# Gate and value products as seven products of sums, in an mLSTM cell with a SwiGLU block

## The chip, the cores and the metric

The kernel runs on one core of one Trainium2 chip. The metric is device time in microseconds of one launch, as the median of several runs. The engines are TensorE (PE: matrix products into PSUM, with its weight loads shown as PEld), VectorE (DVE), ScalarE (ACT), GpSimd (POOL) and SyncE (SP), which here only issues DMAs.

## The reference

An mLSTM cell over 4 batches x 8 heads x 768 steps of 40 features gives y; its rows are laid out as x with 3072 tokens of 320 features. Then a SwiGLU block follows, in float32 throughout:

```python
g = x @ w_gate                            # 320 x 1536
silu = g * (1.0 / (1.0 + np.exp(-g)))
val = x @ w_val                           # 320 x 1536
return (silu * val) @ w_out               # 1536 x 320
```

The weights arrive in 64 bits and are rounded to float32 in the kernel. q, k, v and the gates arrive as float32.

## The kernel before

The 768 steps are cut into six groups of 128 (g = 0 to 5, called groups one to six in the text). A group has 4 batches x 128 steps = 512 tokens. While the SwiGLU block of group g runs on TensorE, the cell of group g+1 is computed in between and the inputs of group g+2 are loaded. Every engine works through its instructions in the order in which the program names them; there is no planner. Lists of closures (`slots`, by chunk, and `before`, by step of the output product) put the cell's parts between the products.

**Gate and value products** (`hidden`, L646). The 1536 hidden features are 12 chunks m of 128. The 320 input features are five pieces of 64 rows. For each piece a gate product runs in rows 0 to 63 of the array and a value product in rows 64 to 127, side by side, each 512 columns wide (L651). The transposed input `xT` therefore holds every piece in both halves. After ten products ScalarE takes the Silu of the gate (L656) and VectorE multiplies it by the value (L657) into `h_sb`.

**Output product** (`project_seven`, L698, from group two on). h and w_out are halved in hidden features, tokens and outputs, and seven half-size products of sums replace eight (L717). The sums of h come from GpSimd (`out_sums`, L688) and VectorE (`out_fourth`, L693); `out_weights` makes those of the weights once, on GpSimd at the start of group two. The first group uses the plain product `project_all` (L664, L668).

**The cell of the next group**: scores (L331) weighed by VectorE (L338); `add` (L353) and `next_state` (L369), with GpSimd's `decayed` (L362); `attend` (L377, L382), then `gather` on VectorE (L391 to L398), GpSimd's `gate` (L403) and `divide` (L409), which writes x. In the slots these come after chunks 3, 4, 5, 7, 8, 9 and 10.

**Turning x.** From group three on, x is sent as 32x32 squares by 16 DMAs per half (`send_squares`, L418) into `x_sq`, and VectorE transposes the squares (`turn_inputs`, L425, L426) into `xT` during the output product, at steps 4 and 5. For groups one and two TensorE transposes x (`first_seam` L558, `seam` L431).

**SP's queue** issues nearly all DMAs, in program order: q and k as squares after chunk 2 (L315), k after 5 (L117), v and the decay weights (`weights_load`, L444) after 9, the o gate after 10, the squares of x after 8 and 10, and the outputs (L709) in the output product. Weights (`piece_load`, L140) come in ten pieces at the start; of the gate and value pieces, gate rows go to partitions 0 to 63 and value rows to 64 to 127, the values by ScalarE's queue for the first five. They are rounded on ScalarE (L190, L192), VectorE (L199, L200) and GpSimd (L207).

PSUM has eight banks, four under the tag "cell" and four under "gen". `hidden` and the output product use "gen", the cell uses "cell".

Of the kernel before, what the change touches and what calls it, by code (L numbers as in the profile page):

```python
# [18 lines left out]
L = 128  # L19
# [5 lines left out]
def kernel(  # L25
# [35 lines left out]
    PAIRS = [(c, c + 1) for c in range(0, NKC - 1, 2)] + [(NKC - 1, 0)] + [(c, c + 1) for c in range(1, NKC - 1, 2)]  # L61
    assert NG * L == S and NFC == 12 and NFC * 128 == DF and TW == 512 and D <= DP and NKC * HP == DM
# [13 lines left out]
    def bank(name, tag="cell"):  # L76
        return psum.tile([128, 512], F32, name=name, tag=tag)
# [16 lines left out]
    vw_sb = const.tile([128, BH, D1], F32)  # L94
# [3 lines left out]
    xT_sb = const.tile([128, NKC, TW], F32, name="xT")  # L98
# [41 lines left out]
    def piece_load(p, home=None):  # L140
        kind, m, n = PIECES[p]
        if kind == "gv":
            a, d = NKC, n * 128
            src = [(slice(i * HP, (i + 1) * HP), w[:, m * 128:(m + n) * 128].rearrange("(c p) f -> p c f", p=HP))
                   for i, w in enumerate((moe_w_gate, moe_w_val))]
            queues = (nc.sync, nc.scalar if p < 5 else nc.sync)
        else:
            a, d = n, DM
            src = [(slice(0, 128), moe_w_out[m * 128:(m + n) * 128].rearrange("(a p) d -> p a d", p=128))]
            queues = (nc.sync,)  # L150
        if src[0][1].dtype == F32:
            for r, w in src:
                if kind == "o":
                    nc.sync.dma_start(out=wo_sb[r, m:m + n, :], in_=w)
                else:
                    for x in range(n):
                        nc.sync.dma_start(out=wgv_sb[r, m + x], in_=w[:, :, ts(x, 128)])
            return
# [5 lines left out]
        for (r, w), queue in zip(src, queues):  # L164
            queue.dma_start(out=raw[r].rearrange("p (a d) -> p a d", a=a), in_=w.bitcast(U32))
# [239 lines left out]
    def divide(n, P, den):  # L405
        for b in range(2):
            u, r = 2 * P + b, slice(b * H, (b + 1) * H)
            x = x_sb[:, u, 0:DM] if n == 1 else x_all[:, u * DM:(u + 1) * DM]
            nc.vector.tensor_tensor(x.rearrange("p (h d) -> p h d", d=D), o_sb[:, u * H:(u + 1) * H],  # L409
                                    den[:, r].to_broadcast([128, H, D]), op=ALU.mult)  # L410
        if n == 1:
            nc.gpsimd.tensor_copy(x_sb[:, 2 * P:2 * P + 2, DM:], x_sb[:, 2 * P:2 * P + 2, 0:HP])

    x_all = x_sb.rearrange("p u d -> p (u d)")[:, 0:B * DM]

    def send_squares(P):  # L418
        for t in range(L // SQ):
            src = x_all[t * SQ:(t + 1) * SQ, 2 * P * DM:(2 * P + 2) * DM].rearrange("p (w e) -> p w e", e=2 * SQ)  # L420
            for r in range(128 // SQ):
                nc.sync.dma_start(out=x_sq[r * SQ:(r + 1) * SQ, 2 * P * NKC:(2 * P + 2) * NKC, t, :],
                                  in_=src[:, :, (r % 2) * SQ:(r % 2 + 1) * SQ])

    def turn_inputs(n, u):  # L425
        nc.vector.transpose(out=xT(n)[:, :, ts(u, L)], in_=x_sq[:, u * NKC:(u + 1) * NKC].rearrange("p w t d -> p w (t d)"))  # L426
# [4 lines left out]
    def seam(n, P, engs):  # L431
        engs = list(engs)
        dst = xT(n).rearrange("p c (u i s) -> p c u i s", u=B, i=2)
        for cs in (range(0, 4), range(4, NKC)):
            tp = [bank("tp_x")[:, 0:len(cs) * L].rearrange("p (c u s) -> p c u s", u=2, s=SUB) for _ in range(2)]
            for c in cs:
                for b in range(2):
                    for i in range(2):
                        nc.tensor.transpose(tp[i][:, c - cs[0], b, :],  # L439
                                            x_sb[half(i), 2 * P + b, ds(PAIRS[c][0] * HP, 2 * HP)], ident[half(i), half(i)])  # L440
            for i in range(2):
                copy(engs.pop(0), dst[:, cs[0]:cs[-1] + 1, 2 * P:2 * P + 2, i, :], tp[i])
# [98 lines left out]
    def first_gate(P):  # L541
# [3 lines left out]
        nc.gpsimd.tensor_copy(x_sb[:, 2 * P:2 * P + 2, DM:], x_sb[:, 2 * P:2 * P + 2, 0:HP])  # L545
# [12 lines left out]
    def first_seam(P, engs):  # L558
        for c, eng in zip(range(0, NKC, 2), engs):
            cs = range(c, min(c + 2, NKC))  # L560
            tp = bank("tp_x")[:, 0:len(cs) * 2 * L].rearrange("p (c u s) -> p c u s", u=2, s=L)
            for w in cs:
                for b in range(2):
                    nc.tensor.transpose(tp[:, w - c, b, :], x_sb[:, 2 * P + b, ds(PAIRS[w][0] * HP, 2 * HP)], ident)
# [36 lines left out]
    first_seam(0, (A, A, V))  # L601
# [5 lines left out]
    first_seam(1, (A, A, V))  # L607
# [38 lines left out]
    def hidden(g, m, first=()):  # L646
        ps = [bank("gv_ps", "gen") for _ in range(2)]
        x = xT(g)
        for kc in range(NKC):
            for i in range(2):  # L650
                nc.tensor.matmul(ps[i], lhsT=wgv_sb[half(i), m, PAIRS[kc][i] if g < 2 else kc, :], rhs=x[half(i), kc, :],  # L651
                                 start=(kc == 0), stop=(kc == NKC - 1))
# [35 lines left out]
    def out_sums(k, eng):  # L688
        eng.tensor_tensor(S1[:, k], h_sb[:, k, second_half], h_sb[:, KH + k, second_half], op=ALU.add)  # L689
        eng.tensor_tensor(h_sb[:, k, second_half], h_sb[:, k, first_half], h_sb[:, k, second_half], op=ALU.subtract)  # L690
        eng.tensor_tensor(S2[:, k], S1[:, k], h_sb[:, k, first_half], op=ALU.subtract)  # L691

    def out_fourth(eng):  # L693
        for k in range(0, KH, 2):
            a12 = h_sb[:, KH + k:KH + k + 2, first_half]
            eng.tensor_tensor(a12, a12, S2[:, k:k + 2], op=ALU.subtract)

    def project_seven(g, before):  # L698
# [5 lines left out]
        node = {x: bank("o_ps", "gen")[:, 0:DM].rearrange("p (u d) -> p u d", d=NW) for x in "eacdb"}  # L704
# [21 lines left out]
        product("e", a12, lambda k: wo_sb[:, KH + k, n1], True, True)  # L726
        step(1)
        product("a", a11, lambda k: wo_sb[:, k, n1], True, True)
        nc.scalar.copy(u2, node["a"])  # L729
        z = fresh()  # L730
        nc.vector.tensor_tensor(z, u2, node["e"], op=ALU.add)  # L731
        send(z, 0, n1)
        out_fourth(nc.vector)
        step(2)
        product("c", a21, lambda k: wo_sb[:, k, n2], True, False)
        nc.scalar.copy(v, node["c"])
# [4 lines left out]
        product("b", lambda k: S2[:, k], lambda k: wT[:, 1, k], True, True)  # L741
# [86 lines left out]
    def early_squares(part):  # L828
# [12 lines left out]
        4: [run(convert, 16), run(seam, 1, 0, (A, V, A, V))],  # L841
        5: [run(seam, 1, 1, (A, V, A, V)), run(convert, 17), run(weights_sub, 2, 0), run(weights_mask, 0)],
# [9 lines left out]
    k_sq = late.tile([128, PP, L // SQ, SQ], F32, name="k_sq")  # L852
    nc.gpsimd.memset(k_sq, 0.0)
    x_sq = late.tile([128, B * NKC, L // SQ, SQ], F32, name="x_sq")
    wT = late.tile([128, 3, KH, NW], F32, name="wT")
    S1 = late.tile([128, KH, TH], F32, name="S1")
    S2 = late.tile([128, KH, TH], F32, name="S2")
    out_weights(nc.gpsimd)

    for g in range(1, NG):  # L860
        n, f = g + 1, g + 2
        slots = {m: [] for m in range(NFC)}
        if n < NG:
            if n > 2:
                slots[0] = [run(turn_squares, q_sq, qT)]
                slots[1] = [run(turn_squares, k_sq, kT)]
            slots[3] = [run(do_scores), run(do_weigh, 0)]
            slots[4] = [run(do_weigh, 1)]
            slots[4].append(run(do_decayed, 2 * n))
            slots[5] = [run(do_add, n), run(do_state, 2 * n)]  # L870
            slots[7] = [run(do_attend, n, 0), run(do_gather, n, 0)]
            slots[8] = [run(do_divide, n, 0), run(send_squares, 0)]
            slots[9] = [run(do_attend, n, 1), run(do_gather, n, 1)]
            slots[10] = [run(do_divide, n, 1), run(send_squares, 1)]
        if f < NG:
            slots[2] += [run(load_squares, q_sq, q, f), run(load_squares, k_sq, k, f)]
            slots[5].append(run(load_all, k_sb, k, f))
# [47 lines left out]
```

## Time and profile before

| | |
|---|---|
| median of 3 runs | 537.5 us (537.4 to 537.51) |
| the profiled execution | 538.14 us |
| its span, first to last instruction | 536.3 us |
| granted TensorE clock | 1.000 |
| busy: PE, PEld | 529.8 us (99%), 338.8 us (63%) |
| busy: DVE, ACT, POOL | 261.0, 132.1, 182.4 us |
| L651, gate and value products | 1440 instructions, 317.2 us |
| L717, output products | 840 instructions |

The span is the time between the first and the last instruction in one profiled execution; the execution lasts a little longer, and the median of runs lies 0.64 us below that one execution. A float32 product is two instructions on TensorE, so the 720 products of L651 are 1440. Matmul durations overlap: a line's busy time counts a stretch once, its mean duration is that of one instruction alone.

### The profile page before, as it was taken

The numbers are of one execution on the slowest core, as the hardware profiler recorded it, in microseconds if no ns is written. First come the engines' busy times: TensorE is split into PE (matmuls) and PEld (weight loads), VectorE is DVE, ScalarE is ACT, GpSimd is POOL, SyncE is SP. The second block draws the span as 40 slices with busy tenths as digits, with TensorE's granted clock in tenths as the row PEclk, the third lists the DMA queues.
The fourth block names the chain that finished last, engine by engine and source line by source line (L and its number), as shares of the span: only waits on it lengthen the run. The fifth ranks groups of instructions, "written<-read, shape, count | busy, mean of one in ns | idle before, by whom it ended". The sixth has DMA issues, their size and how long they took to land.

```text
span 536.3 us, 12510 instructions
## 1 busy us (share of the span) xinstructions
PE 529.8 (99%) x5349; PEld 338.8 (63%) x5349; DVE 261.0 (49%) x437; ACT 132.1 (25%) x193; POOL 182.4 (34%) x194
## 2 busy tenths in 40 slices
PE   8999999999999999999999999999999999999997
PEld 4964545766745697555598455589455579544496
DVE  5769686982255542545633436635435734111121
ACT  3367555444110114101013210104201010011110
POOL 1303346579216534014627004437003530003410
PEclk9999999999999999999999999999999999999999
DMA  9999997898640496471296353296000131000001
GB/s 125 175 275 197 183 286 144 155 122 125 74 55 1 73 137 116 50 88 17 46 149 131 45 58 51 38 150 113 26 2 2 26 60 41 24 1 0 2 12 38
DMA packets 226879, 45.76 MB, mean 85 GB/s; under 512 B 214824, under 2 KB 221992, under 8 KB 226824
## 3 DMA queue, kind: packets, MB, share of 16 engines
q1 hardware_dynamic: 224916, 42.11, 48.9%
q10 hardware_dynamic: 1908, 2.85, 2.0%
q8 instruction: 42, 0.69, 0.6%
q14 instruction: 13, 0.11, 0.1%
HBM read 35.68 MB, written 4.01 MB: 74 GB/s over the span
## 4 chain that ended last, share of the span: by engine, by line
PE 91%; DMA 4%; SPq 3%; DVE 1%; POOL 0%; issue 0%; DVEq 0%; POOLq 0%
PE gv_ps L651 56%; PE o_ps L717 21%; PE o_ps L668 5%; SPq L117 3%; DMA wo_sb<-in_moe_w_gate_dram 2%; PE inter L377 2%; PE sp L331 2%; PE intra L382 2%; DMA raw<-in_moe_w_gate_dram 2%; PE add L353 2%; PE tp_kq L296 0%; POOL wgv_sb L207 0%; DVE M_sb L281 0%; PE tp_x L439 0%; DVE wgv_sb L200 0%
## 5 line engine op out<-in xcount | busy, mean ns | idle before, releaser
L651 PE MATMUL gv_ps<-xT,wgv_sb 64*128 64x512 f32 x1440 | 317.2, 593 | 0.9 <-DVE wgv_sb L207 0.8
L651 PEld LDWEIGHTS gv_ps<-xT,wgv_sb 64*128 64x128 f32 x1440 | 142.3, 187 | 155.2 <-issue 148.9
L657 DVE TENSOR_TENSOR h_sb<-sg,gv_ps 128x512 f32<-128x512 f32 x72 | 49.4, 686 | 177.3 <-ACT sg L656 177.3
L656 ACT ACTIVATE sg<-gv_ps 128x512 f32<-128x512 f32 x72 | 43.0, 597 | 264.8 <-PE gv_ps L651 264.6
L717 PEld LDWEIGHTS o_ps<-wo_sb,h_sb 128*128 128x128 f32 x480 | 65.6, 190 | 3.8 <-issue 3.8
L717 PE MATMUL o_ps<-wo_sb,h_sb 128*128 128x160 f32 x480 | 67.4, 300 | 0.0
L689 POOL TENSOR_TENSOR S<-h_sb 128x256 f32<-128x256 f32 x30 | 23.2, 773 | 100.9 <-DVE h_sb L657 100.9
L362 POOL TENSOR_TENSOR C<-C,dec 128x328 f32<-128x328 f32 x20 | 14.5, 736 | 114.6 <-DVE C L369 114.6
L456 POOL TENSOR_SCALAR_AFFINE_SELECT w_sb<-w_sb 64x1024 f32<-64x1024 f32 x20 | 28.4, 1421 | 37.1 <-DVE w_sb L451 36.1
L717 PE MATMUL o_ps<-wT,S 128*128 128x160 f32 x240 | 33.4, 299 | 0.0
L717 PEld LDWEIGHTS o_ps<-wT,S 128*128 128x128 f32 x240 | 32.9, 190 | 0.0
L668 PE MATMUL o_ps<-wo_sb,h_sb 128*128 128x320 f32 x96 | 26.9, 437 | 0.0
L690 POOL TENSOR_TENSOR h_sb<-h_sb 128x256 f32<-128x256 f32 x30 | 22.8, 760 | 2.4
L668 PEld LDWEIGHTS o_ps<-wo_sb,h_sb 128*128 128x128 f32 x96 | 17.9, 190 | 7.2
L691 POOL TENSOR_TENSOR S<-S,h_sb 128x256 f32<-128x256 f32 x30 | 21.7, 724 | 0.0
L394 DVE TENSOR_TENSOR y_sb<-y_sb,intra 64x328 f32<-64x328 f32 x40 | 19.7, 492 | 0.7
L369 DVE TENSOR_TENSOR C<-C,add 40x328 f32<-40x328 f32 (+1 forms) x36 | 17.7, 493 | 1.2 <-POOL C L362 0.6
L207 POOL TENSOR_TENSOR wgv_sb<-wgv_sb,low 128x640 int32<-128x640 int32 x6 | 9.3, 1544 | 24.6 <-DVE wgv_sb L200 24.6
L717 PE MATMUL o_ps<-wT,h_sb 128*128 128x160 f32 x120 | 17.1, 299 | 0.0
L731 DVE TENSOR_TENSOR z_sb<-sg,o_ps 128x320 f32<-128x320 f32 x5 | 2.4, 487 | 29.3 <-ACT sg L729 23.5
L426 DVE STREAM_TRANSPOSE xT<-x_sq 128x640 f32<-128x640 f32 x16 | 12.5, 822 | 8.5 <-DMA x_sq<-x_sb 8.5
L717 PEld LDWEIGHTS o_ps<-wT,h_sb 128*128 128x128 f32 x120 | 16.6, 190 | 0.0
(152 smaller groups left out, 471.8 us busy)
## 6 DMA issues: line engine op xcount, KB each, us to landing
w_sb<-M_dram SPq DMA_DIRECT2D x10, 512.0 KB, 11.3
x_sq<-x_sb SPq DMA_DIRECT2D x128, 40.0 KB, 2.0
k_sb<-in_k_dram SPq DMA_DIRECT2D x12, 320.0 KB, 6.0
v_sb<-in_v_dram SPq DMA_DIRECT2D x12, 320.0 KB, 5.8
o_sb<-in_o_gate_dram SPq DMA_DIRECT2D x12, 320.0 KB, 5.5
raw<-in_moe_w_out_dram SPq DMA_DIRECT2D x3, 1280.0 KB, 7.4
q_sb<-in_q_dram SPq DMA_DIRECT2D x32, 64.0 KB, 2.3
out_dram<-z_sb SPq DMA_DIRECT2D x20, 80.0 KB, 2.5
```

Source lines behind the costliest of these rows:

```text
L117: nc.sync.dma_start(out=dst[:, heads(P), 0:D], in_=tokens(a, c, P))
L369: nc.vector.tensor_tensor(c, c, ps[r], op=ALU.add)
L394: nc.vector.tensor_tensor(t, t, intra[i][half(c)], op=ALU.add)
L456: nc.gpsimd.affine_select(w, w, compare_op=ALU.is_ge, fill=NEG, base=0, pattern=[[0, UH], [1, SUB]], channel_multiplier=-1)
L651: nc.tensor.matmul(ps[i], lhsT=wgv_sb[half(i), m, PAIRS[kc][i] if g < 2 else kc, :], rhs=x[half(i), kc, :], start=(kc == 0), stop=(kc == N ...
L656: nc.scalar.activation(sg, ps[0], AF.Silu)
L657: nc.vector.tensor_tensor(hid(g, m), sg, ps[1], op=ALU.mult)
L668: nc.tensor.matmul(ps[u], lhsT=hid(g, m)[:, ts(u, L)], rhs=wo_sb[:, m, :], start=(m == 0), stop=(m == NFC - 1))
L689: eng.tensor_tensor(S1[:, k], h_sb[:, k, second_half], h_sb[:, KH + k, second_half], op=ALU.add)
L690: eng.tensor_tensor(h_sb[:, k, second_half], h_sb[:, k, first_half], h_sb[:, k, second_half], op=ALU.subtract)
L691: eng.tensor_tensor(S2[:, k], S1[:, k], h_sb[:, k, first_half], op=ALU.subtract)
L717: nc.tensor.matmul(node[x][:, i], lhsT=lhs(k)[:, ts(i, L)], rhs=rhs(k), start=start and k == 0 and i == 0, stop=stop and k == KH - 1, skip ...
```

## The change

1. `hidden` (groups one and two) takes 256 features as full-height products of 128 rows, and the remaining 64 as a pair of 64-row products, gate in the upper half of the array and value in the lower. Even chunks end with the pair, odd chunks begin with it. x's last 64 features stand in both halves of `xT`'s third block; the other features are stored once, so `xT` has 3 blocks for 5, the seams transpose 3 for 5, and each square DMA carries 6 for 10 pieces. The weights of a piece come in four DMAs for two.
2. In groups three to six `unit` does chunks k and k+6 together. The 256 features, gate/value and the 512 tokens are halved, and seven 128-row products of 256 columns per chunk replace eight; the 64-row rest is done plainly in 64-row pairs, four products per chunk. ScalarE copies the first node, VectorE adds five times from PSUM and multiplies twice, ScalarE takes two Silus of 512 columns (as before).
3. The weight sums are made once, by GpSimd during group two, after each chunk; two DMAs swap the halves of the 64-row weights. The input sums are five VectorE operations per group, after the turns.
4. The output product has four nodes for five; the sum S2 is formed in place by VectorE (`out_second`).
5. Units and cell steps take the two PSUM tags in turn.
6. Moved: the turns of q and k from chunks 0 and 1 of the next group to step 1 of the output product, and with them k's load; k's squares after chunk 6 for 2; v's load from after chunk 9 to after the second half of x's squares; all four turns of x at step 4.

The diff, cut to its core:

```diff
+        src = [(slice(0, 128), slice(2 * i, 2 * i + 2), w[0:256, cols].rearrange("(c p) f -> p c f", p=128), queue)
+               for i, (w, queue) in enumerate(((moe_w_gate, nc.sync), (moe_w_val, second)))]
+        src += [(half(i), slice(4, 5), w[256:DM, cols].rearrange("(c p) f -> p c f", p=HP), nc.sync)
+                for i, w in enumerate((moe_w_gate, moe_w_val))]
...
     def hidden(g, m, first=()):
...
-        for kc in range(NKC):
-            for i in range(2):
-                nc.tensor.matmul(ps[i], lhsT=wgv_sb[half(i), m, PAIRS[kc][i] if g < 2 else kc, :], rhs=x[half(i), kc, :],
-                                 start=(kc == 0), stop=(kc == NKC - 1))
+        for part in ((0, 1) if m % 2 == 0 else (1, 0)):
+            opens, closes = part == m % 2, part != m % 2
+            for c in range(2) if part == 0 else (2,):
+                for i in range(2):
+                    w, r = (wgv_sb[:, m, 2 * i + c], x[:, c]) if part == 0 else (wgv_sb[half(i), m, 4], x[half(i), 2])
+                    nc.tensor.matmul(ps[i], lhsT=w, rhs=r, start=opens and c != 1, stop=closes and c != 0)
...
+    def out_second(eng):
+        for k in range(0, KH, 2):
+            a11 = h_sb[:, k:k + 2, first_half]
+            eng.tensor_tensor(a11, S1[:, k:k + 2], a11, op=ALU.subtract)
...
+    def weight_sums(ms, eng):
+        w, t = wgv_sb[:, ms], wS[:, ms]
+        eng.tensor_tensor(t[:, :, 0], w[:, :, 2], w[:, :, 3], op=ALU.add)
+        eng.tensor_tensor(t[:, :, 1], t[:, :, 0], w[:, :, 0], op=ALU.subtract)
+        eng.tensor_tensor(t[:, :, 2], w[:, :, 1], t[:, :, 1], op=ALU.subtract)
...
+    def input_sums(eng):
+        x1, x2 = (lambda c: xT_sb[:, c, first_half]), (lambda c: xT_sb[:, c, second_half])
+        eng.tensor_tensor(xT_sb[half(1), 2, second_half], xT_sb[half(1), 2, second_half], xT_sb[half(1), 2, first_half],
+                          op=ALU.subtract)
+        eng.tensor_tensor(xS[:, 0], x2(0), x1(0), op=ALU.subtract)
+        eng.tensor_tensor(xS[:, 1], x2(1), xS[:, 0], op=ALU.subtract)
+        eng.tensor_tensor(x2(0), x2(1), x2(0), op=ALU.subtract)
+        eng.tensor_tensor(xS[:, 2], x1(1), xS[:, 1], op=ALU.subtract)
+
+    def unit(k, tag):
+        ms = (k, KH + k)
+        A4 = [bank("gv_ps", tag).rearrange("p (j t) -> p j t", j=2) for _ in range(4)]
+        na, nb, nd, ne = A4
...
+        rest = xT_sb[:, 2]
+        for two in (((na, 0, wgv_sb[:, :, 4], rest[:, first_half]), (nb, 1, wR, rest[:, second_half])),
+                    ((nd, 0, wR, rest[:, second_half]), (ne, 1, wgv_sb[:, :, 4], rest[:, second_half]))):
+            for j, m in enumerate(ms):
+                for node, i, w, x in two:
+                    nc.tensor.matmul(node[:, j], lhsT=w[half(i), m], rhs=x[half(i)], start=j == 0, stop=False,
+                                     skip_group_check=True)
+
+        def product(node, w, x, stop):
+            for j, m in enumerate(ms):
+                nc.tensor.matmul(node[:, j], lhsT=w(m), rhs=x, start=False, stop=stop, skip_group_check=True)
...
+        product(na, lambda m: wgv_sb[:, m, 0], x1(0), False)
+        nc.scalar.copy(sa, na)
+        product(nb, lambda m: wS[:, m, 1], xS[:, 1], True)
+        nc.vector.tensor_tensor(sa, sa, nb, op=ALU.add)
+        product(nd, lambda m: wgv_sb[:, m, 2], x2(0), False)
+        nc.vector.tensor_tensor(h2, sa, nd, op=ALU.add)
+        product(ne, lambda m: wS[:, m, 0], xS[:, 0], False)
+        nc.vector.tensor_tensor(h2, h2, ne, op=ALU.add)
+        product(na, lambda m: wgv_sb[:, m, 1], x1(1), True)
+        nc.scalar.activation(sg, na, AF.Silu)
+        product(nd, lambda m: wgv_sb[:, m, 3], xS[:, 2], True)
+        nc.vector.tensor_tensor(h1, sa, nd, op=ALU.add)
+        nc.vector.tensor_tensor(h1, sg, h1, op=ALU.mult)
+        product(ne, lambda m: wS[:, m, 2], x2(1), True)
+        nc.vector.tensor_tensor(sa, sa, ne, op=ALU.add)
+        nc.scalar.activation(sa, sa, AF.Silu)
+        nc.vector.tensor_tensor(h2, sa, h2, op=ALU.mult)
+        out_sums(k, nc.gpsimd)
...
     for g in range(1, NG):
...
-            slots[2] += [run(load_squares, q_sq, q, f), run(load_squares, k_sq, k, f)]
-            slots[5].append(run(load_all, k_sb, k, f))
-            slots[9] += [run(load_all, v_sb, v, f), run(weights_load, f)]
-            slots[10].append(run(load_all, o_sb, o_gate, f))
-        for m in range(NFC):
-            hidden(g, m)
-            if m >= KH:
-                out_sums(m - KH, nc.gpsimd)
-            for s in slots[m]:
-                s()
+            slots[2] += [run(load_squares, q_sq, q, f)]
+            slots[6] += [run(load_squares, k_sq, k, f)]
+            slots[9] += [run(weights_load, f)]
+            slots[10] += [run(load_all, v_sb, v, f), run(load_all, o_sb, o_gate, f)]
+        if g == 1:
+            for m in range(NFC):
+                hidden(g, m)
...
+                weight_sums(slice(m, m + 1), nc.gpsimd)
+                weight_difference(slice(m, m + 1), nc.gpsimd)
+            weight_rest(nc.gpsimd)
+        else:
+            for j in range(KH):
+                unit(j, side())
+                for s in slots[2 * j] + slots[2 * j + 1]:
+                    s()
...
-            before[4] += [run(turn_inputs, n, 0), run(turn_inputs, n, 1)]
-            before[5] += [run(turn_inputs, n, 2), run(turn_inputs, n, 3)]
+            before[4] += [run(turn_inputs, n, u) for u in range(B)] + [run(input_sums, nc.vector)]
+            before[1] += [run(turn_squares, q_sq, qT), run(turn_squares, k_sq, kT), run(load_all, k_sb, k, f)]
```

## The prediction

> **What bounds it now.** I read, in this order, the busy table, the chain that ended last, then the timelines of VectorE and of SP's queue over the third group (208.3 to 291.5 us), because the change hands work to exactly those two.
>
> ```profile
> PE 529.8 (99%) x5349; PEld 338.8 (63%) x5349; DVE 261.0 (49%) x437; ACT 132.1 (25%) x193; POOL 182.4 (34%) x194
> PE 91%; DMA 4%; SPq 3%; DVE 1%; POOL 0%; issue 0%; DVEq 0%; POOLq 0%
> ```
>
> TensorE is busy throughout, and beyond the first 46 us the chain stays on it. So each PE microsecond removed counts, until another queue makes PE wait. The chain in order of time (start, length, engine, tile, line, instructions) gives PE's rates:
>
> ```profile
> 99.32 8.81 PE o_ps L668 x32
> 108.13 0.77 PE tp_x L439 x20
> 108.90 2.35 PE o_ps L668 x8
> ...
> 374.74 17.37 PE gv_ps L651 x80
> 392.11 2.02 PE sp L331 x128
> 394.13 8.78 PE gv_ps L651 x40
> ...
> 434.82 23.02 PE o_ps L717 x168
> 457.84 51.70 PE gv_ps L651 x240
> ```
>
> A float32 matmul is two instructions. Take a chunk m of L651 (20 instructions, ten pairs of 64-row halves) as a, a start as t: 240 take 12a+t = 51.70, 80 take 4a+t = 17.37; so a = 4.291 us and **t = 0.205 us**. L668 says the same: 32c+t = 8.81, 8c+t = 2.35, c = 0.2692, t = 0.197. Each such start is a change of how the array is cut (64 rows to 128, or 64x64 to 64x128). For L717, (23.02-0.2)/168 = 0.1358. Hence 135.8 ns at 160 columns, 269.2 at 320 and 429.1 per 64-row pair at 512: a column over 1.2 GHz, plus 2.5 ns. At 256 columns I use **215.8 ns**.
>
> **PE, part by part.** A unit replaces two chunks (8.58 us). It has 16 rest instructions in 8 pairs, 8 x 0.2158 = 1.73, and 7 products of 4, 28 x 0.2158 = 6.04: 7.77 us. It saves 0.81; 24 units (groups three to six) save 19.5 us.
>
> Against that stand the new changes of cut, 0.2 each. Each unit changes once inside (rest to products): 6 per group. The first two units stand side by side, one more; before each cell step a change was there already; the project step now follows 128-row work, one less. That is +1.2 us in groups three to five. Group six has no cell steps: 6+5-1 = 10, +2.0. Together 5.6: **PE net -13.9 us**.
>
> In groups one and two the products stay whole, now 128-row plus a 64-row pair (8 x 0.4292 + 2 x 0.4292 = a again), with a change inside each chunk: 12 x 0.2. Group two saves those at its two ends, less the small rest: +1.8. In group one PE waits for weights up to the fourth chunk (45.9 us), which hides those; eight chunks and the key/query turns remain: +1.9. The seam into group two turns 24 instead of 40 blocks (two 0.77 rows to 0.46): -0.6. The new loading of the weights (four DMAs per piece for two) I take as 0, bounded by +-1.5: the third chunk's weights arrive at 38.1 us and PE waits 0.56 for them; the bytes are the same, but eight outstanding DMAs hold half as many pieces.
>
> A rule of the Trainium skill speaks against the whole plan: "TensorE: Matmul & The Clock Gate", Part 3, The mechanism, says that a weight load overlaps running matmuls only where their row groups differ. By that, 28 loads of 0.19 us would stand bare in each unit, 128 us in all. L717's row contradicts it: 480 full-height loads of 190 ns each, one matmul every 137 ns; the measurement decides.
>
> **VectorE inside a unit.** Rows: 128x512 with a PSUM operand 0.686 (L657; next independent start after 0.61), ScalarE 0.60 (L656). With PE starting at 0, rest and two changes end at 2.13, then 0.863 per product: na 2.99, nb 3.86, nd 4.72, ne 5.58, na 6.45, nd 7.31, ne 8.17. VectorE: first add 3.9-4.6, second 4.75-5.4, third 5.6-6.3; then add, product, add, ScalarE's Silu, product: 7.35 to 10.7. It falls 2.5 us behind PE's end, but its next first add is due at 8.17+3.9 = 12.07. So **units in a row don't stall** (group six). PE needs the second add by 6.45, which is the tight place. Around it stand the cell's steps:
>
> ```profile
> 237.85 4.09 DVE L369 TENSOR_TENSOR C<-C,add 40x328 f32<-40x328 f32 x8
> ...
> 248.20 0.90 DVE L391 TENSOR_TENSOR y_sb<-inter,e_T 128x328 f32<-128x328 f32 x2
> 249.01 2.06 DVE L394 TENSOR_TENSOR y_sb<-y_sb,intra 64x328 f32<-64x328 f32 x4
> 251.11 0.19 DVE L396 SCALAR_TENSOR_TENSOR den<-y_sb 128x16 f32<-128x16 f32 x1
> 251.33 1.34 DVE L397 TENSOR_SCALAR den<-den 128x16 f32<-128x16 f32 x1
> 252.71 0.25 DVE L398 RECIPROCAL den<-den 128x16 f32<-128x16 f32 x1
> ...
> 254.71 1.42 DVE L409 TENSOR_TENSOR x_sb<-o_sb,den 128x320 f32<-128x320 f32 x2
> ```
>
> All of these now queue behind a unit's last product and ahead of the next unit's first add. From group start (PE at 0): third unit ends 26.5, VectorE 29.1; state 4.1 plus GpSimd's decays behind its two sums ends at 33.5; the fourth unit's first add was due at 32.0, its PE stalls 0.4. Fourth unit ends 36.7, gather (0.9+2.06+1.85 from 39.2) 43.8 against 42.5: stall 0.2. Fifth unit ends 47.0, its VectorE 49.5; divide to 50.9, second gather to 55.6 against 52.9: stall 1.6. Sum 2.2 per group, three groups: **+6.5 us** (1 to 4 each). Units end at 58.8, the project step (22.8) at 81.6.
>
> **The seam: SP's queue.** The same queue carries the inputs' squares, the next group's loads and the outputs.
>
> ```profile
> 256.15 11.85 SPq L422 DMA_DIRECT2D x_sq<-x_sb  x16
> 268.11 2.22 SPq L117 DMA_DIRECT2D v_sb<-in_v_dram  x2
> 270.42 3.78 SPq L447 DMA_DIRECT2D w_sb<-M_dram  x2
> 274.30 13.09 SPq L422 DMA_DIRECT2D x_sq<-x_sb  x16
> 287.48 1.67 SPq L117 DMA_DIRECT2D o_sb<-in_o_gate_dram  x2
> 289.25 2.05 SPq L709 DMA_DIRECT2D out_dram<-z_sb  x2
> 291.39 0.85 SPq L709 DMA_DIRECT2D out_dram<-sg  x2
> ```
>
> Before, the last squares are issued at 287.4, VectorE turns them by 290.8 and PE starts the next group at 291.48: 0.7 us to spare. SP had no gap from 256.2 on, so SP, not PE, nearly sets this seam already.
>
> After: the first divide comes after the fifth unit, so squares start at 51.6 (50.9, then GpSimd's copy). 16 issues 11.9 -> 63.5. Then the weights' two loads and 16 issues: 16.9 as above with v's two loads queued ahead of them; these are moved behind, so 13.4 (2.2 for two loads on an empty queue, as v's row, and 16 x 0.657+0.7). End T = 76.9. Landing 1.9 (median 2.0), two turns 1.0, first of the input sums 0.4: 80.2, before PE's 81.6. So the inputs come in time.
>
> But behind T now stand **six** loads of 320 KB (v, o, and k, whose buffer the squares of k occupy until the turn), and only then z's and v's outputs. In the changed program's order the next unit's first ScalarE copy takes over the buffer that v's output is sent from. A load lasts 1.74 us at the 188 GB/s of 270.4 to 274.3 us: 10.5 for six; with first byte, z's and v's pairs (0.9 each, partly beneath) and 1.7 landing, v's output is gone between T+12.4 and T+14; I take T+13.2 = 90.1, copy done 90.7. PE starts the unit at 81.6 and needs that copy before the fifth product, at 87.2: stall 3.5, and 0.5 more as the second add is late. 4.0 at the seams after groups three and four: **+8.0**. After group two T is 75.5 and PE's need 90.7 (its groups are longer): 0. After group five nothing is loaded: 0.
>
> What costs nothing: the weight sums on GpSimd in group two (48 of 128x128, about 0.4 each by L412's 0.49, against 0.77 for 128x256: 20 us) lie beneath 60 us of PE, 0 to +1 where a state decay queues behind one; the added swap of 64-row weights, two DMAs, has the whole of group two; out_second's and the inputs' sums, 3 x 0.68 and 5 x 0.35 on VectorE, lie in 22.8 us of project, whose VectorE has 8 us more left.
>
> The skill's "TensorEngine Tiling (Array Packing)", PSUM Bottleneck, warns that faster TensorE work moves the limit to emptying PSUM. Here VectorE's 7 against 2 passes per unit are 4.8 of 8.2 us, and only cell steps tip it; by the rule every unit would be bound by VectorE, by my rows three of six in three groups.
>
> **The sum.** -13.9 +1.8 +1.9 -0.6 +6.5 +8.0 = +3.7 us on the profiled execution's 538.14 (span 536.3): 541.8. The runs' median is 0.64 below that execution: **541.2**.
>
> **Rivals.** (1) **Squares are issued faster**: each DMA moves 192 pieces instead of 320. If its 0.613 us goes with that (0.37) or even to 0.49 as q's squares, T comes 4 us earlier, v's output is out in time, and the 8.0 is gone: 533.2, faster. It decides from T = 73. Against: w_out's DMAs, with more pieces, take 0.38, q's 512 take 0.49; the number of pieces doesn't set the time. For: nothing else has this shape. (2) **VectorE's passes are dearer** (0.8 for 0.686, two SBUF operands beside GpSimd): stalls 4.2 per group, and the seam no later: 547. (3) **The change of cut costs nothing inside one accumulation**: 9 us less, 532. (4) PE's sum without any stall: 526.7. (5) GpSimd or the weights' loads hold the first two groups: 545 to 555.
>
> **Chances.** Forecast 0.42; rival 1 0.30; 2 0.12; 3 0.07; 4 0.02; 5 0.07. Faster by over 0.2% (1.1 us, about what this measurement tells from none): 0.38; within: 0.08, where forecast and rival 1 meet halfway; slower: 0.54. Signs are mixed: the forecast's own range is 538 to 546, the whole 530 to 549.
>
> **What would show it.** Right: units of 8.2 us in group six; first unit of groups four and five near 12 us with ScalarE waiting for a DMA of sg; sixth units near 9.8. Wrong: x_sq issues far below 0.6; a weight wait beyond 46 us; PE idle in the middle of group six.

## The result and the profile after

The changed kernel takes **571.73 us** (569.0 to 574.43, four runs) where the kernel before takes 537.5: a ratio of 1.0635 [1.0569, 1.07]. I had forecast 541.2 with a range of 530 to 549. Its runs lie 5.4 us apart, those of the kernel before 0.6. The profiled execution took 569.0 us, its span is 567.2, 30.9 more than before.

The page of the changed kernel, first the busy times, then the clock granted to TensorE in 40 slices, then the shares of the chain that ended last:

```profile
PE 539.0 (95%) x5229; PEld 409.0 (72%) x5229; DVE 357.2 (63%) x585; ACT 147.4 (26%) x218; POOL 189.3 (33%) x220
...
PEclk9999999999999999999998898889979999999999
...
PE 62%; SPq 14%; DVE 10%; DMA 6%; POOL 3%; issue 2%; ACT 2%; DVEq 0%; ACTq 0%; POOLq 0%
```

PE is busy for 95% of the span and not 99%, and yet its busy time rose by 9 us although it has less to do. The line of the clock says where to look: in six of the slices 22 to 30 (298 to 425 us) it is below full speed, which it never was before. The mean over the span is 0.976, a figure that looks harmless. The chain, 91% PE before, now runs for 14% through SP's queue and for 10% through VectorE.

Where the 30.9 us lie, by the start of each group's first gate and value product:

| stage | before, us | after, us | difference | my sum |
|---|---|---|---|---|
| up to group two's products | 125.06 | 126.58 | +1.5 | +1.3 |
| group two | 83.28 | 85.39 | +2.1 | +1.8 |
| group three | 83.14 | 85.22 | +2.1 | -1.5 |
| group four | 83.19 | 105.20 | +22.0 | +2.5 |
| group five | 83.10 | 89.16 | +6.1 | +2.5 |
| group six to the end | 78.53 | 75.65 | -2.9 | -2.9 |

The first two rows and the last came out as forecast; groups three to five did not, and group four holds over two thirds of the loss. PE's five largest waits, by what released them (total, times, longest, in us):

```profile
PE gv_ps L748 <- ACT sg L754: 11.2, 3, 6.1
PE gv_ps L748 <- DVE h_sb L758: 4.3, 7, 1.6
PE gv_ps L743 <- DVE y_sb L397: 2.7, 2, 2.0
PE gv_ps L743 <- DVE C L375: 1.6, 3, 1.0
PE gv_ps L655 <- ACT xT L125: 1.6, 1, 1.6
```

The first row is the seam that I had forecast: the first unit's ScalarE copy (L754) is late, because the buffer sg is still being sent out. The second is VectorE's second addition, forecast too. Rows three and four are new: a unit's first products wait for VectorE to finish with y_sb and C, which belong to the cell. The chain in order of time (start, length, engine, tile, line, instructions) shows what these waits draw behind them:

```profile
302.68 0.75 ACT o_sb L464
303.43 0.96 SPq L783
305.39 2.77 DMA out_dram<-sg
308.91 5.49 PE gv_ps L748 x12
314.39 2.20 PE gv_ps L743 x16
316.59 6.24 PE gv_ps L748 x28
...
339.13 3.17 PE gv_ps L743 x8
342.29 7.06 PE gv_ps L748 x24
...
491.62 1.93 PE gv_ps L743 x16
493.55 6.24 PE gv_ps L748 x28
```

In group six 28 instructions of L748 take 6.24 us, 0.22 each. Behind the wait that ends at 308.9, 12 of them take 5.49, 0.46 each: **half speed**. At 339 it happens again. The same is seen when the span is cut into stretches; a row holds the stretch, its length, the busy time of PE, PEld, DVE, ACT and POOL, then the granted clock, the DMA share and GB/s:

```profile
308.08:314.91 6.83, 6.00 (x14) 4.33 (x16) 3.92 (x6) 2.47 (x3) 0.00 (x0) 0.50 0.69 94
338.81:345.63 6.82, 6.55 (x17) 4.48 (x17) 1.25 (x3) 0.59 (x1) 0.00 (x0) 0.50 0.69 76
355.87:359.29 3.42, 3.42 (x11) 2.39 (x11) 1.60 (x2) 0.00 (x0) 1.34 (x1) 0.50 0.02 5
369.52:372.94 3.42, 3.42 (x15) 2.95 (x14) 3.26 (x7) 0.00 (x0) 1.29 (x2) 0.50 0.23 38
410.49:417.31 6.82, 5.83 (x14) 4.23 (x16) 3.74 (x6) 2.47 (x3) 0.00 (x0) 0.50 0.12 37
```

Five stretches, each 3.41 us long or twice that, all at 0.50. PE works for 25.2 us of their 27.3, so half speed cost, by this estimate, some 12.6 us beside the waits themselves. That is the largest single term, and I had none for it.

### The profile page after: what moved, and what is told of

Read it like the earlier page. It is cut to its first block, busy times and chain, and to the rows that moved or that the text cites. A ratio compares the mean times of both kernels' runs of the same rounds, so it can differ in the third digit from the quotient of the medians.

```text
span 567.2 us, 12646 instructions
## 1 busy us (share of the span) xinstructions
PE 539.0 (95%) x5229; PEld 409.0 (72%) x5229; DVE 357.2 (63%) x585; ACT 147.4 (26%) x218; POOL 189.3 (33%) x220
## 4 chain that ended last, share of the span: by engine, by line
PE 62%; SPq 14%; DVE 10%; DMA 6%; POOL 3%; issue 2%; ACT 2%; DVEq 0%; ACTq 0%; POOLq 0%
PE gv_ps L748 20%; PE gv_ps L655 19%; PE o_ps L791 9%; SPq L425 7%; PE gv_ps L743 6%; SPq L121 5%; PE o_ps L671 5%; DMA o_sb<-in_o_gate_dram 3%; PE sp L337 2%; DMA h_sb<-in_moe_w_gate_dram 1%; SPq L783 1%; DVE y_sb L400 1%; DMA out_dram<-sg 1%; DVE h_sb L764 1%; DVE h_sb L765 1%
## 5 line engine op out<-in xcount | busy, mean ns | idle before, releaser
L655 PE MATMUL gv_ps<-xT,wgv_sb 128*128 128x512 f32 (+1 forms) x288 | 111.2, 609 | 1.6 <-ACT xT L125 1.6
L748 PE MATMUL gv_ps<-xT,wgv_sb 128*128 128x256 f32 x288 | 80.3, 403 | 11.2 <-ACT sg L754 11.2
L655 PEld LDWEIGHTS gv_ps<-xT,wgv_sb 128*128 128x128 f32 (+1 forms) x288 | 43.1, 188 | 60.9 <-issue 56.8
L748 PEld LDWEIGHTS gv_ps<-xT,wgv_sb 128*128 128x128 f32 x288 | 54.6, 197 | 27.6 <-ACT sg L754 12.4
L743 PE MATMUL gv_ps<-xT,wgv_sb 64*128 64x256 f32 x192 | 52.4, 412 | 3.7 <-DVE y_sb L397 2.7
L743 PE MATMUL gv_ps<-xT,wR 64*128 64x256 f32 x192 | 51.9, 413 | 1.1 <-DVE C L375 0.6
L748 PE MATMUL gv_ps<-xS,wS 128*128 128x256 f32 x192 | 50.0, 384 | 0.0
L743 PEld LDWEIGHTS gv_ps<-xT,wgv_sb 64*128 64x128 f32 x192 | 35.7, 198 | 10.7 <-issue 4.8
L748 PEld LDWEIGHTS gv_ps<-xS,wS 128*128 128x128 f32 x192 | 37.2, 194 | 5.3
L743 PEld LDWEIGHTS gv_ps<-xT,wR 64*128 64x128 f32 x192 | 35.5, 198 | 4.6 <-issue 1.7
L754 ACT COPY sg<-gv_ps 128x512 f32<-128x512 f32 x24 | 14.1, 587 | 95.1 <-PE gv_ps L748 77.7
L659 ACT ACTIVATE sg<-gv_ps 128x512 f32<-128x512 f32 x24 | 14.4, 598 | 67.7 <-PE gv_ps L655 67.7
L768 ACT ACTIVATE sg<-sg 128x512 f32<-128x512 f32 x24 | 15.1, 630 | 64.4 <-DVE sg L767 64.4
L748 PE MATMUL gv_ps<-xS,wgv_sb 128*128 128x256 f32 x96 | 27.1, 408 | 4.3 <-DVE h_sb L758 4.3
```

What stands on the lines that cost most here:

```text
L655: nc.tensor.matmul(ps[i], lhsT=w, rhs=r, start=opens and c != 1, stop=closes and c != 0)
L743: nc.tensor.matmul(node[:, j], lhsT=w[half(i), m], rhs=x[half(i)], start=j == 0, stop=False, skip_group_check=True)
L748: nc.tensor.matmul(node[:, j], lhsT=w(m), rhs=x, start=False, stop=stop, skip_group_check=True)
L768: nc.scalar.activation(sa, sa, AF.Silu)
```

## The experiments

**Theory A**: PE stands still for reasons of queues and buffers, and the clock is halved because it stood still. **Theory B**, the rival: the clock is halved because the new products are denser, and the waits count for themselves alone.

**1 and 2. Each wait by itself, then both.** Group four's waits have a cause that I had read wrongly. Scores take a PSUM tag beside the unit's, as I wrote; but state and attends get their banks from a helper whose tag is fixed:

```python
def small(name, n=UA, tag="cell"):
```

In groups three and five most units use gen; in group four, since a group takes 11 turns, they use cell, the same four banks as the state and attends between them:

```profile
334.34 1.39 PE L359 MATMUL add<-vx_sb,k_sb 64*40 64x41 f32 x62 [0.49 <-DVE sg L767]
336.73 0.67 PE L743 MATMUL gv_ps<-xT,wgv_sb 64*128 64x256 f32 x2 [1.00 <-DVE C L375]
...
353.31 0.70 PE L743 MATMUL gv_ps<-xT,wgv_sb 64*128 64x256 f32 x2 [0.66 <-DVE y_sb L397]
...
369.20 0.94 PE L743 MATMUL gv_ps<-xT,wgv_sb 64*128 64x256 f32 x2 [1.99 <-DVE y_sb L397]
```

The last bracket is the wait ahead of the row and who ended it: a unit cannot begin until VectorE has emptied the cell's banks.

```diff
-    def small(name, n=UA, tag="cell"):
+    def small(name, n=UA, tag=None):
...
-        place["cell"] = side()
+        place["cell"] = side() if live.get("units") else "cell"
```

> One edit: the cell's state and attend products take the PSUM tag that the unit beside them does not use (in the changed kernel they always take the tag cell, which the units of group four take too, so PE waits there for VectorE to empty the cell's banks). Theory A, bank waits plus a clock that is halved after PE has waited: group four loses the waits that group three does not have (5.5 - 2.0 = 3.5 us), the three half-clock stretches after 335 us (13.65 us at half speed, 6.6 us lost) and about 3 us of late VectorE behind them: 13 us less, 556 us where the changed kernel's fastest run has 569; only the half-clock stretches behind the two seams stay, mean clock 0.988. Theory B, the clock is halved by the denser products themselves, not by waiting: only 3.5 us less, 565, and half-clock stretches in the middle of groups stay.

Measured: 558.27 us (ratio to before 1.0388 [1.0371, 1.0405]), 13.5 below the changed kernel; clock 0.990. Between the seams only waits of 0.2, 0.2 and 1.6 us are left in group four, and there the clock is 1.00 throughout; the half-clock stretches behind two seams stay:

```profile
306.86:313.68 6.82, 4.79 (x11) 3.82 (x12) 2.93 (x5) 2.47 (x3) 0.00 (x0) 0.50 0.72 125
335.00:379.00 44.00, 42.06 (x485) 36.80 (x482) 38.80 (x63) 6.72 (x12) 11.48 (x14) 1.00 0.35 53
399.02:402.43 3.41, 2.86 (x7) 2.27 (x8) 2.06 (x3) 2.38 (x3) 0.00 (x0) 0.50 0.06 16
```

The products are the same, so their density alone did not halve the clock in group four. A's number is met, B's isn't.

```diff
-            slots[10] += [run(load_all, v_sb, v, f), run(load_all, o_sb, o_gate, f)]
...
-            before[1] += [run(turn_squares, q_sq, qT), run(turn_squares, k_sq, kT), run(load_all, k_sb, k, f)]
+            before[1] += [run(turn_squares, q_sq, qT), run(turn_squares, k_sq, kT)]
...
+            before[5] += [run(load_all, o_sb, o_gate, f), run(load_all, v_sb, v, f), run(load_all, k_sb, k, f)]
```

> One edit: the loads of o, v and k for the next group but one are issued after v's output in step 5 of the output product, not ahead of all outputs. Theory A: ScalarE's first copy of the next group no longer waits for the output's DMA, PE's 11.2 us of waits for it go, and with them the two half-clock stretches behind the seams (about 12 us at half speed, 5.9 lost): 17 us less, 552 us, unless o's later landing holds ScalarE's sigmoid ahead of that copy (up to 1 us per seam). Theory B: 11 us less, 558, and the clock is still halved at the same places.

> Both edits. Theory A: the waits of both kinds and all half-clock stretches go, groups three to five take about 82.5 us each: 569 - 30 = 539 us, mean clock 1.000, within 3 us of the kernel before. Theory B: 554 us, clock below 1.

Measured: 568.46 us (1.0561 [1.0513, 1.061]) for the loads alone, 552.95 (1.0271 [1.0231, 1.0311]) for both. The first is 3.3 us better and not 17, the second 14 us worse than A expected: **my account of the seam was incomplete**. SP's queue and ScalarE at the seam, with both edits:

```profile
294.96 1.01 SPq L783 DMA_DIRECT2D out_dram<-z_sb  x2
301.04 0.81 SPq L783 DMA_DIRECT2D out_dram<-sg  x2
301.89 1.85 SPq L121 DMA_DIRECT2D o_sb<-in_o_gate_dram  x2
```

```profile
305.74 0.74 ACT L464 ACTIVATE o_sb<-o_sb 128x640 f32<-128x640 f32 x1 [7.57 <-DMA o_sb<-in_o_gate_dram]
307.52 0.74 ACT L464 ACTIVATE o_sb<-o_sb 128x640 f32<-128x640 f32 x1 [1.05 <-DMA o_sb<-in_o_gate_dram]
308.16 0.57 ACT L754 COPY sg<-gv_ps 128x512 f32<-128x512 f32 x1
```

SP stands for 5 us before it can send v's output: GpSimd's last sum for it comes after VectorE's turns and input sums. The loads now wait behind that, o lands at 305.7, and its sigmoids stand ahead of the first copy on ScalarE. In the changed kernel these sigmoids had ended at 303.4, and the buffer held the copy until 308.2; here the sigmoids end at 308.2 and hold it. So the edit put one wait in the place of the other: PE stands 4.2 us at this seam for 6.1.

**3. Is it the standing still?** The kernel before, which has no sums and no half clock, got five made pauses in group six:

```diff
             hidden(g, m)
+            if g == 5 and m in PAUSES:
+                t, u = w_sb[:, 0:8], w_sb[:, 8:16]
+                for i in range(PAUSES[m]):
+                    nc.scalar.copy(u if i % 2 == 0 else t, t if i % 2 == 0 else u)
+                last_t = t if PAUSES[m] % 2 == 0 else u
+                nc.tensor.matmul(bank("pause")[:, 0:64], lhsT=last_t[:, 0:2], rhs=last_t[:, 2], start=True, stop=True)
```

> The kernel before with five made pauses of TensorE in group six, after chunks 1, 3, 5, 7 and 9: a small product waits for a chain of 1, 2, 4, 6 and 9 copies of 128x512 on ScalarE that starts behind the chunk's Silu. Nothing else of the kernel changes. By ScalarE's 0.6 us per pass the pauses are about 1.5, 2.1, 3.4, 4.6 and 6.5 us, 18 in all. Theory A: the longer pauses are followed by one or two stretches of 3.41 us at half clock: 537.5 + 18 + 5 to 10 = 560 to 566 us, mean clock 0.97 to 0.98. Theory B: 537.5 + 18 = 556 us and clock 1.000.

Measured: 564.8 us in one run, clock 0.985. The pauses (last bracket), and below them the stretches with their clock:

```profile
467.36 0.43 PE L888 MATMUL pause<-w_sb 128*128 128x64 f32 x2 [1.19 <-ACT w_sb L886]
478.42 0.43 PE L888 MATMUL pause<-w_sb 128*128 128x64 f32 x2 [1.84 <-ACT w_sb L886]
490.77 0.43 PE L888 MATMUL pause<-w_sb 128*128 128x64 f32 x2 [3.13 <-ACT w_sb L886]
506.12 0.69 PE L888 MATMUL pause<-w_sb 128*128 128x64 f32 x2 [4.43 <-ACT w_sb L886]
524.74 0.69 PE L888 MATMUL pause<-w_sb 128*128 128x64 f32 x2 [6.38 <-ACT w_sb L886]
```

```profile
462.00:470.00 8.00, 6.81 (x34) 2.94 (x32) 1.38 (x2) 1.66 (x3) 0.00 (x0) 1.00 0.00 0
491.87:495.28 3.41, 3.41 (x10) 1.39 (x8) 0.00 (x0) 0.00 (x0) 0.00 (x0) 0.50 0.00 0
505.52:512.35 6.83, 6.23 (x16) 3.04 (x18) 0.00 (x0) 0.55 (x1) 0.00 (x0) 0.50 0.00 0
522.59:529.41 6.82, 4.67 (x12) 2.37 (x14) 0.00 (x0) 2.00 (x4) 0.00 (x0) 0.50 0.01 2
```

1.2 and 1.8 us leave the clock alone; 3.1, 4.4 and 6.4 us are followed by 3.41 or 6.83 us at half. Theory B is out as the cause: here no denser product exists. The Trainium skill, "TensorE: Matmul & The Clock Gate", Part 1, What's actually happening, states this: a free-running window of 3.413 us, at whose end an idle array falls to half clock. The lengths agree; but it speaks of a whole idle window, and here less was enough: the third pause fills only 2.3 us of the 3.41 that end at 491.87.

The counter-test in the changed kernel: leave the waits, but let PE work through them.

```diff
+        if fill:
+            t = bank("fill", {"cell": "gen", "gen": "cell"}[tag])
+            for _ in range(fill):
+                nc.tensor.matmul(t, lhsT=wgv_sb[:, 0, 0], rhs=xT_sb[:, 0], start=True, stop=True)
         product(na, lambda m: wgv_sb[:, m, 1], x1(1), True)
```

> The changed kernel with products that nobody reads (128x512, 0.86 us each) put into the first unit of groups three, four and five, 2, 7 and 4 of them, just ahead of the product that waits for ScalarE's copy: TensorE works through the wait (1.7, 6.1 and 3.4 us) and then goes on as before. No wait is removed. Theory A, the clock is halved because TensorE stood still: the half-clock stretches behind the seams (308 and 410 us) go, those in the middle of group four stay: 569 - 5.5 = 563.5 us. Theory B, it is halved by the products' density: all stretches stay or get longer, 569 or more.

Measured: 567.12 us (1.0528 [1.0499, 1.0556]), 4.6 below the changed kernel, where A had 5.5. Behind the seams of its profiled execution the clock is now 1.00, while group four's waits are still followed by half clock:

```profile
303.00:312.00 9.00, 9.00 (x39) 5.80 (x36) 1.00 (x3) 1.48 (x2) 3.38 (x3) 1.00 1.47 167
312.00:320.00 8.00, 7.48 (x36) 4.71 (x35) 4.67 (x7) 3.10 (x4) 0.00 (x0) 1.00 0.74 125
410.00:420.00 10.00, 9.82 (x45) 6.31 (x44) 4.71 (x7) 3.10 (x4) 0.00 (x0) 1.00 0.31 72
339.62:349.86 10.24, 10.24 (x28) 7.00 (x29) 3.40 (x7) 0.58 (x1) 1.86 (x3) 0.50 0.58 64
373.75:377.17 3.42, 3.42 (x11) 2.30 (x10) 1.48 (x2) 0.00 (x0) 1.19 (x1) 0.50 0.23 37
```

The copy comes late as before, TensorE has more work, and the time is shorter: theory A. (The gain is that of the medians; this execution, 569.46 us, also lost time to 6.83 us of half clock near its start, which the shown one of the changed kernel did not have.) The row of 10.24 us shows something that A does not explain: three half-clock windows in a row in which PE never stood still. What starts half clock is shown; what keeps it for one, two or three windows is not.

**4. The other parts without the seven products.**

```diff
-        if g == 1:
+        if True:
             for m in range(NFC):
                 hidden(g, m)
...
-                weight_sums(slice(m, m + 1), nc.gpsimd)
...
-            before[4] += [run(turn_inputs, n, u) for u in range(B)] + [run(input_sums, nc.vector)]
+            before[4] += [run(turn_inputs, n, u) for u in range(B)]
```

> The changed kernel without its seven products: groups three to six take the gate and value products whole, by hidden as groups one and two do (no sums of weights or inputs, cell steps on the tag cell, products on gen as before the change). The inputs stored once, the new weight loading, the four nodes of the output product and the moved loads and turns stay. My terms: +3.1 us in groups one and two, and a change of cut in each of 48 more chunks, 9.6, less about 1.6 for the ends that lay at a change already: 537.5 + 11 = 548 us, no wait at the seams since the units' VectorE passes do not delay the squares, clock 1.000. If moving the loads behind the squares were itself what holds the seams, waits for ScalarE and half clock would be here too, 555 or more.

Measured: 553.52 us (1.0287 [1.026, 1.0314]), no wait of PE above 0.2 us after 40 us. So the other parts cost 16 us by themselves; the seven products, with VectorE's waits, win 12.4 of them back in v1_seams below (14.4 by groups three to six of the two profiled executions). Twelve chunks of group six take 53.9 us for 51.5: the change of cut inside each chunk, 0.2, as computed. The run is 5.5 us above what I expected, and most of that lies ahead of group two: its products start at 129.97, 4.9 later than before the change, where I had 1.3. That led to the next finding.

**5. The start.** In the changed kernel ScalarE's queue reads (start, length, instruction, wait ahead of it):

```profile
28.71 0.80 ACT L198 ACTIVATE low<-raw 128x640 int32<-128x640 uint32 x1
31.44 0.38 ACTq L171 DMA_DIRECT2D h_sb<-in_moe_w_val_dram  x1
31.85 0.59 ACT L125 COPY xT<-tp_x 128x512 f32<-128x512 f32 x1 [2.35 <-DMA h_sb<-in_moe_w_gate_dram]
```

Before the change the same load was issued at 28.33, without a wait. Each of the 388 DMAs of this trace reports its landing by one of eight semaphores, and they are used in turn. A piece now takes four DMAs for two, so the eight come round sooner, and ScalarE may not issue its load before an earlier one of the same semaphore has landed (SP's of 23.71, at 31.42). Behind it stands the copy into xT that PE's first product needs: 1.6 us in this execution, 2.2 and 3.2 in those of v1_seams and e6_off, where 3.41 us at half clock follow (from 33.04 and 35.44 us).

```diff
-    piece_load(3, h_sb[:, NH - NKC:])
     join(0)
     first_seam(1, (A, V))
+    piece_load(3, h_sb[:, NH - NKC:])
```

> The changed kernel with one move near its start: the loads of the fourth piece of weights are issued after the second half of the first group's inputs is turned, not ahead of it. In the changed kernel ScalarE's own load of that piece waits for one of eight DMA semaphores (each piece now takes four DMAs, not two), and behind it stands ScalarE's copy into xT that TensorE's first product needs: PE waits 1.6 us at 32 us in the shown execution and 2.2 to 3.2 us in other kernels of this study, where a half-clock stretch at 33 to 39 us follows. Theory A: the wait and the early half clock go, the second group starts 1.7 us earlier than in the shown execution and up to 4 us earlier than in others; the median falls from 571.7 by 2 to 4 us and the rest stays. Theory B: the weights themselves land late, which the order does not change: the wait moves to the copy's place in the chain of the next chunk, median as before.

Measured: 571.31 us (1.062 [1.0576, 1.0663]). No difference: the wait for the copy is gone, but in that execution the weights came late instead (2.5 us of waits for them), and the changed kernel's spread hides 2 us. Alone it settles nothing; in a version without the other waits it does (v3_first, next).

**6. Versions that take all of it away.** v1_seams has its own tags for the cell, a buffer of its own for v's output, and the sigmoids behind the first copy. v2_gather also moves a gather, v3_first adds the move of experiment 5 to v1, v4_shift also runs the cell one unit earlier:

```diff
-        kept = {x: work.tile([128, TW], F32, name="sg")[:, 0:DM].rearrange("p (u d) -> p u d", d=NW) for x in "uv"}
+        kept = {"u": work.tile([128, TW], F32, name="sg")[:, 0:DM], "v": v_own}
...
         nc.scalar.copy(sa, na)
+        for f in copied:
+            f()
...
+            copied[0] = [run(sig, 0), run(sig, 1)]
```

> Own tags for the cell as in e1_side; v's output gets a buffer of its own; ScalarE's sigmoids of the o gate come behind the first unit's copy instead of ahead of it. The loads stay where the change put them. Theory A: nothing of the seam stands ahead of the first copy any more, its waits (2, 6 and 3.5 us) and every half-clock stretch go; what stays is VectorE's 2.2 us per group and groups one and two: e3_both's 549 less 9.2 of waits and 3.4 of half clock, 536 us, equal to the kernel before within 0.5%. If another wait (the sigmoids' load of a function table, the inputs' turns) takes their place: 540 to 548.

> As v1_seams, and the second gather of the cell is put behind the third addition of the sixth unit instead of ahead of that unit, so that VectorE serves the products first. Theory A: the 1.6 us wait of each sixth unit goes, the output product may wait 0.6 us for the last unit's products instead: 3 us below v1_seams, 533 us. If the squares are held up by as much as the gather comes later, the gain is given back at the seam: as v1_seams.

Measured: v1 541.15 us (1.0063 [1.005, 1.0075]), v2 541.7 (1.0067 [1.0042, 1.0092]). The seam waits and every half-clock stretch after 40 us are gone in both. v1 is 5 us above A's number, by an error of mine: I took e3_both's waits, read from its profiled execution of 552.9 us, off its fastest run. From the same execution the sum is 552.9 - 12.6 = 540.3. Its start is slow too: group two begins at 128.84. In v2 the sixth units no longer wait; the output product does:

```profile
PE o_ps L796 <- DVE h_sb L769: 4.3, 3, 1.5
PE gv_ps L748 <- DVE h_sb L760: 1.2, 6, 0.2
```

VectorE had too much to do between the fifth unit and the output product, and changing the order within that stretch only moved the wait.

```diff
+            e = 2 if g > 1 else 0
-            slots[5] = [run(cell, do_add, n), run(do_state, 2 * n)]
+            slots[5 - e] = [run(cell, do_add, n), run(do_state, 2 * n)]
...
+            if g > 1:
+                added[4] = first_squares
...
+            slots[10 - e // 2] += [run(do_divide, n, 1), run(send_squares, 1)]
```

> v1_seams with the same move. Theory A: 541.2 less 2 to 4 us: 538, equal to the kernel before within 0.3%, clock 1.000 until the end in most runs. What is left against my sum of -13.9 us is VectorE's 2 us in each of three groups and the changes of cut in groups one and two.

> v3_first with the cell's steps of groups three to five one unit earlier (scores behind the first unit, state behind the second, attends behind the third and fourth), the first divide behind the third addition of the fifth unit and the second behind the fifth unit, so that no unit has a divide and a gather of VectorE ahead of its additions. Theory A: the 1.6 us wait of the sixth units goes, 0.2 to 0.4 us per cell step stay: 4 us below v3_first, 533.5 to 534.5, 0.7% below the kernel before. If v and k land too late for the earlier steps, or the squares too late for the seam, new waits for DMA or GpSimd show at the second unit or at the group's start: 538 or more.

Measured: v3 537.21 us (0.9998 [0.9984, 1.0012]), 3.9 below v1: the start is worth what I expected (group two begins at 125.59), and the version equals the kernel before. v4 **534.56 us (0.9935 [0.9921, 0.995])**, 0.65% below the kernel before: little, but its interval lies wholly below 1. Its page:

```profile
PE 524.0 (98%) x5227; PEld 399.7 (75%) x5229; DVE 353.7 (66%) x585; ACT 147.0 (28%) x218; POOL 188.6 (35%) x220
...
PEclk9999999999999999999999999999999999999999
```

By stage against the kernel before: +1.0 to group two, +2.6, then -1.9, -1.5, -1.5 for groups three to five and -2.9 at the end.

**7. Why did 1.1 us suffice in group four?** There 1.1 to 2.0 us of waiting in a 3.41 us stretch halved the clock; one of 1.6 us among full products did not, in any kernel here.

> The kernel before with 13 made pauses of one kind (a small product waits for four copies on ScalarE, about 1.7 us): eight straight behind the cell's attends of groups two to five, whose products are 64x64 with 41 columns, and five between whole chunks of group six. It tests why waits of 1.1 to 2.0 us inside group four of the changed kernel were followed by half clock, while one of 1.6 us ahead of the sixth unit's last products was not. If what counts is how much of the array worked in a stretch of 3.41 us (the small products count little): most of the eight are followed by half-clock stretches (each 1.7 us lost) and none of the five, 537.5 + 22 + about 10 = 570 us. If what counts is the standing time alone, the two kinds come out alike: none of them halves (560 us), or both do.

Measured: 588.4 us in one run, clock 0.971. The test was badly made: the five controls lasted 2.9 us, not 1.7, and put 2.1 to 2.7 us of standing into one window of 3.41; all were followed by half clock, so they don't compare with the eight. Of the eight pauses of 1.64 us behind attends, four were followed by 3.41 us at half and four were not. That fits a count of how much of the array worked (the pauses of experiment 3 and the waits of 1.6 us in e1_side, all among full products, halved nothing up to 1.8 us), but no run separates it from other readings: why the same pause is hit four times of eight, and the threshold, stay open.

## Why the prediction was wrong, point by point

- **PE per unit: right.** 1.93 + 6.24 = 8.17 us, six units without a wait in group six, -2.9 us there. The Trainium skill's "TensorEngine Tiling (Array Packing)", PSUM Bottleneck, says only that emptying PSUM may become the limit; I had read it as if it bound every unit. By these rows no unit is bound unless the cell's work comes between. Missed: in groups three and five the state's 128 products take 2.05 and 2.09 us where they took 1.6 (0.4 per group). Why is open: in group two they take 1.48, and there too full-height products stand ahead of them.
- **Groups one and two: group two right (+2.1 for +1.8); what lies ahead of it right in sum, by luck.** The new loading of the weights, "0, bounded by +-1.5", is mis-sized: v1 against v3 gives 3.9 us. The shown execution began group two at 126.58, others with the same start at 126.3 (e1_side) to 130.95 us (e5_fill). I had written that eight outstanding DMAs hold half as many pieces, but not asked which engine issues the ninth and what stands behind it.
- **VectorE inside units: right in groups three and five.** L748's 28 take 6.31 us undisturbed in group three, 6.79, 6.80 and 8.15 in the last three units: 2.8 lost for the 2.2 forecast. **Wrong in group four**: I took "Units and cell steps take the two PSUM tags in turn" from the diff, without following the helper that most cell steps call. 5.2 us of waits, 13.5 with what followed.
- **The seam: the mechanism right, its size too small.** ScalarE waits for the DMA of sg, as forecast. The squares end at 81.1 us after the group's start (forecast 76.9; some 3 of the 4.2 are late units), the output is gone 15.1 us later (forecast 13.2). So waits of 1.7, 6.1 and 3.4 us, where I had 0, 4 and 4. And e2_sends and e3_both show that sending the loads later does not cure it: v's sum and the sigmoids are late as well.
- **The step that failed: a microsecond of waiting was priced at one microsecond.** Every term with a wait assumed a TensorE that goes on at full speed. Half clock cost some 12.6 us in the profiled execution; e4_pause and e5_fill show that standing still is what brings it. PE's busy share of 99% before the change had hidden that this price exists. Of the 27.2 us between my sum (+3.7) and the span (+30.9), 12.6 are half clock, 5.2 the bank waits of group four, which I had at nothing, and 3 to 4 the seams beyond the 8.0; some 4 us of group four I cannot assign. In v1_seams, without the bank and seam waits, group four takes no longer than group three (82.6 us each).
- **Rivals.** The squares were not issued faster (0.60 to 0.61 us each). VectorE's passes are 0.69 as in the row. The change of cut does cost 0.2 (e6_off). The fifth rival, a start held by the weights, had 0.07 and was real in part.

## What to carry to other kernels

On a TensorE that was never idle, waits of 2 us or more cost up to twice themselves here: look at the granted clock by stretches, not at its mean, and price each new wait with the half-clock window behind it. Follow every helper that hands out a buffer to its default tag before you call two uses apart. Where a queue's order is moved, ask of each engine what stands behind an instruction that now waits, the DMA that a computing engine issues included.

## What the runs showed of the hardware

- Half clock comes in stretches of 3.41 us or multiples. Among full-size products at full clock, standing times up to 1.83 us within such a window (301.26 to 304.67 in the changed kernel) left the clock alone, and 2.08 us or more (505.28 to 508.69 in e8_beside) halved it; among small products 1.1 us could do it. At half clock less is needed for a second window: 0.6 us (505.52 to 508.93 in e4_pause), in group four none at all (339.62 to 349.86 in e5_fill).
- The same waits are hit differently from run to run: two runs of the changed kernel had a mean clock of 0.976 and took 569.0 and 569.5 us, two had 0.970 and took 573.9 and 574.4. Group four's waits between the seams brought 13.7 us of half clock in the changed kernel and 20.5 in e7_first, which has the same code there.
- A unit that waits 0.2 us for VectorE inside its products loses 0.5 us (6.79 for 6.31).
